# A three-layer kernel whose first stage becomes one written list of single-engine steps, with the retention state summed in PSUM

## The chip, the cores and the metric

One core of a Trainium2 chip runs the kernel. The metric is the device time in microseconds (us) of one execution; a lower number is better. Engine names are those of the profile: PE is TensorE (PEld its weight loads), DVE VectorE, ACT ScalarE, POOL GpSimd, SP SyncE, which here issues almost all DMA transfers. One profiled execution gives the durations, and three unprofiled runs give the times.

## The reference

The input is q, k, v of 4 sequences x 8 heads x 576 positions x 64 dimensions, and the weights of two dense layers.

```python
gamma = 1.0 - 2.0 ** (-5.0 - np.arange(H))            # one decay per head
Dmat = np.where(rel >= 0, gamma ** rel, 0.0)          # rel = position of q - position of k
x = (q @ k.T / sqrt(D) * Dmat) @ v                    # retention; 2304 tokens x 512
h = x @ w_in                                          # 512 -> 1024
solu = h * softmax(h)
ln = (solu - mean) / sqrt(var + 1e-6) * g_ln
x = ln @ w_out                                        # 1024 -> 512
h = x @ w_in2                                         # 512 -> 2048
g = where(h >= 1, h, where(h <= -1, 0, (h + 1)**2 / 4))
out = g @ w_out2                                      # 2048 -> 512
```

The weights arrive as 64-bit floating point words. The chip's engines take them apart as pairs of 32-bit integers ("decoding") and each number is then split into a high and a low part; a product is the sum of three matmuls (low-high, high-low, high-high).

## The kernel before, in words

The 2304 tokens are 18 tiles of 128; a sequence is 4.5 tiles, so tile number modulo 9 is 0 or 4 where a sequence begins, and in tile 4 it begins in the middle.

The kernel has two stages. The **first stage** holds the retention (`ret_scores`, `ret_out`), the first dense layer with its normalisation (`mlp1_hidden`, `mlp1_norm`, `mlp1_transpose`), its output product (`mlp1_out`), and the decoding of all weights: `prep_w_in1` and `prep_w_out1` for the first layer, `prep_w2` for the second layer, whose split weights are stored to DRAM. The **second stage** begins behind the last tile's transposes (`hidden`, `factors`, `project`) and loads these weights again for each block of 512 tokens.

Retention of a tile: PE makes the scores of two heads at a time (L117), DVE multiplies them by a table `in_sb` of decays that is zero above the diagonal (L126), POOL multiplies q by a table (L130) and k by another (L133). PE adds the state of earlier tiles (L145) and the tile's own part (L151) in one PSUM bank `po`, which ACT and DVE split into high and low (L74, L75 by `split`). The next state is the old one times a decay (POOL L182, or ACT L174) plus k times v (PE L172 into a bank `pst`, DVE L185; L179 where a sequence begins). The state lies in SBUF.

First layer of a tile: 12 matmuls of 512 columns for each half of the hidden units (L252), the maximum (DVE L257), exponential (ACT L267), product (DVE L268), squares (ACT L275), the inverse root (POOL L281, L282), scaling (ACT L285), 8 transposes (PE L298), a split, and for each pair of tiles 96 matmuls of 256 columns (L318).

Decoding of one unit of 128 x 512 numbers: ACT scales the high words (L199) and the low words (L200), DVE shifts (L201), POOL adds (L202), DVE merges (L204), ACT and DVE or POOL split. There are 48 such units, of which 16 belong to the first layer.

What sets the order: up to tile 3's hidden half the string `START` gives the order of calls, then a loop over pairs of tiles, with `PACE` as the number of weight units between the calls. Only the queues of SP (in `START`), and of PE and SP (afterwards), keep the written order (`manual_schedule`); on the other engines a planner orders the instructions with its own costs. The 8 PSUM banks are four pairs named `sc`, `o`, `tr`, `h`, each reused in turn.

Of the kernel before, what the change touches and what calls it, by code (L numbers as in the profile page):

```python
# [31 lines left out]
PACE = [[], [0, 0, 0, 0], *[[2, 1, 1, 1]] * 4, *[[2, 2, 1, 1]] * 2, [0, 0, 0, 0]]  # L32

START = """
L0 G0 L1 s0 A0 G1 O0 S1 L2 o1 A1 L3 S2 o2 A2 L4 S3 A3 O3 L5 S4 B0 O4 L6 S5 b1 O5 L7 B2 S6 O6 H0 H1 L8 b3 S7 O7 N0 L9 B4 S8 O8 b5 H2 H3 L10 S9 O9 N1 B6 b7 L11
# [3 lines left out]
def shape_constants():  # L39

    gamma = 1.0 - 2.0 ** (-5.0 - np.arange(H, dtype=np.float64))
    g = gamma.reshape(KD, 2).T
    i = np.arange(P)
    lag = (i[None, :] - i[:, None])[:, None, None, :]
    inside = np.where(lag >= 0, g[None, :, :, None] ** np.maximum(lag, 0), 0.0) / np.sqrt(D)
    before = np.repeat(g[:, :, None] ** (i + 1.0) / np.sqrt(D), D, 0)
    after = gamma[None, :] ** (P - 1.0 - i[:, None])
    across = np.repeat(g ** float(P), D, 0)  # L50
    return [np.ascontiguousarray(x, np.float32) for x in (inside, before, after, across)]
# [3 lines left out]
def net(ctx: ExitStack, tc: tile.TileContext, qk_t, kv, w_in1, w_out1, g_ln, w_in2, w_out2, inside, before, after, across, out):  # L55
# [5 lines left out]
    ps = mlp1.enter_context(tc.tile_pool(name="ps", bufs=2, space=PSUM))  # L61
# [4 lines left out]
    small = ctx.enter_context(tc.tile_pool(name="small", bufs=4, side="right"))  # L66
# [19 lines left out]
    in_sb = at.tile([P, 2, KD, P], F32, name="in_sb", bufs=1)  # L86
    bef_sb = at.tile([P, KD, P], F32, name="bef_sb", bufs=1)
    aft_sb = at.tile([P, H], F32, name="aft_sb", bufs=1)
    acr_sb = at.tile([P, KD], F32, name="acr_sb", bufs=1)
    state = at.tile([P, KD, P], F32, name="state", bufs=1)  # L90
    nc.gpsimd.memset(state, 0.0)
    raws, scaled, x1, probs = {}, {}, {}, {}

    def load_inside(e):
        nc.sync.dma_start(in_sb[:, e], inside[:, e])

    def load_consts(i):
        for x, src in (((aft_sb, after), (bef_sb, before)), ((acr_sb, across), (g_sb, g_ln)))[i]:
            nc.sync.dma_start(x, src)

    def load_qkv(t):
        x = raw.tile([P, 2, KD, P], F32, tag="qk", name="qk")
        y = raw.tile([P, 2, H, D], F32, tag="kv", name="kv")
        nc.sync.dma_start(x, qk_t[t])
        for e in range(2 if t == 0 else 0):
            load_inside(e)
        nc.sync.dma_start(y, kv[t])
        raws[t] = x, y

    def ret_scores(t, alt=False):  # L110
        r = t % RPT
        qk, kv_ = raws[t]
        sc = [ps.tile([P, KD, P], F32, tag="sc", name=f"sc{e}") for e in range(2)]
        for c in range(KD):
            for e in range(2):
                rows = slice(e * D, (e + 1) * D)
                nc.tensor.matmul(sc[e][:, c, :], qk[rows, 1, c, :], qk[rows, 0, c, :], start=True, stop=True)  # L117
        for e in range(2):
            pt = at.tile([P, KD, P], F32, tag=f"p{e}", name=f"p{e}", bufs=1)
            if r == 4:  # L120
                nc.gpsimd.memset(pt[:D, :, D:], 0.0)
                parts = ((slice(0, D), slice(0, D)), (slice(D, P), slice(0, P)))
            else:
                parts = ((slice(0, P), slice(0, P)),)
            for j, i in parts:
                nc.vector.tensor_tensor(out=pt[j, :, i], in0=sc[e][j, :, i], in1=in_sb[j, e, :, i], op=ALU.mult)  # L126
            probs[t, e] = pt
        if r:
            qs = at.tile([P, KD, P], F32, tag="qs", name="qs")
            nc.gpsimd.tensor_tensor(out=qs, in0=qk[:, 0, :, :], in1=bef_sb, op=ALU.mult)  # L130
            scaled[t] = qs
        if r != RPT - 1:
            (nc.vector if alt else nc.gpsimd).tensor_tensor(  # L133
                out=kv_[:, 0, :, :], in0=kv_[:, 0, :, :], in1=aft_sb.unsqueeze(2).to_broadcast([P, H, D]), op=ALU.mult
            )

    def ret_out(t, alt=False):
        r = t % RPT
        _, kv_ = raws.pop(t)
        po = ps.tile([P, KD, P], F32, tag="o", name="po")  # L140
        n_in = 0 if r == 0 else D if r == 4 else P
        if n_in:
            qs = scaled.pop(t)
        for c in range(KD if n_in else 0):
            nc.tensor.matmul(  # L145
                po[:, c, :n_in], state[:, c, :], qs[:, c, :n_in], start=(c == 0), stop=False, skip_group_check=True
            )
        for c in range(KD):
            for e in range(2):
                rows = slice(e * D, (e + 1) * D)  # L150
                nc.tensor.matmul(  # L151
                    po[rows, c, :], kv_[:, 1, 2 * c + e, :], probs[t, e][:, c, :],
                    start=(c == 0 and n_in == 0), stop=(c == KD - 1), skip_group_check=True,
                )
# [7 lines left out]
        xh, xl = x[:, 0], x[:, 1]  # L162
        split(xh, xl, po)
        x1[t] = (xh, xl)
        if r != RPT - 1:
            k0 = D if r == 4 else 0
            pst = ps.tile([P, KD, P], F32, tag="o", name="pst")
            kf = kv_[:, 0, :, :].rearrange("p h d -> p (h d)")
            vf = kv_[:, 1, :, :].rearrange("p h d -> p (h d)")
            for c in range(KD):  # L170
                cols = slice(c * P, (c + 1) * P)
                nc.tensor.matmul(pst[:, c, :], kf[k0:, cols], vf[k0:, cols], start=True, stop=True)  # L172
            for c in range(KD if alt and r not in (0, 4) else 0):
                nc.scalar.activation(state[:, c, :], state[:, c, :], AF.Copy, scale=acr_sb[:, c : c + 1])  # L174
            for e in range(2):
                rows = slice(e * D, (e + 1) * D)
                st = state[rows, :, rows]
                if r in (0, 4):
                    nc.vector.tensor_copy(st, pst[rows, :, rows])  # L179
                    continue  # L180
                if not alt:
                    nc.gpsimd.tensor_tensor(  # L182
                        out=st, in0=st, in1=acr_sb[rows, :].unsqueeze(2).to_broadcast([D, KD, D]), op=ALU.mult
                    )
                nc.vector.tensor_tensor(out=st, in0=pst[rows, :, rows], in1=st, op=ALU.add)  # L185
# [6 lines left out]
    def decode(st, tag=None, sb=False, dst=None):  # L192

        lo, hi = st[:, :, 0], st[:, :, 1]
        y = stage.tile([P, 512], U32, tag="y", name="y", bufs=3)
        w = ps.tile([P, 512], U32, tag=tag, name="w") if tag else y
        nc.scalar.activation(w.bitcast(F32), hi.bitcast(F32), AF.Copy, scale=2.0**-112)  # L199
# [442 lines left out]
```

## Time and profile before

| | us |
|---|---|
| three runs | 722.74, 725.28, 725.74 |
| median of the runs | 725.28 |
| the profiled execution, span from its first to its last instruction | 723.5 |
| a time of its own for the profiled execution, beside its span | not given |
| start of tile 16's transposes, with which the second stage begins | 326.64 |

In windows a line gives each engine's busy time with the count of its instructions, then the granted clock of TensorE as a share of its full speed, the share of the DMA engines' time and the rate. A group of instructions names line, engine, operation and tiles; "x36 | 24.4, 684" is 36 instructions, 24.4 us busy, 684 ns for a mean one; behind the second bar stands the engine's idle time before them and what ended it.

### The profile page before, as it was taken

How to read it: one execution, taken by the hardware profiler on the slowest of the kernel's cores; microseconds unless marked ns; L12 is line 12 of the kernel's file. 1: busy time of each engine (PE TensorE's matmuls, PEld its weight loads, DVE VectorE, ACT ScalarE, POOL GpSimd, SP SyncE). 2: the span in 40 equal slices, each digit the busy share in tenths (PEclk: the TensorE clock that was granted, in tenths of full speed). 3: DMA queues.
4: the chain of work that ended last, by engine and by line, in shares of the span. 5: the costliest groups of instructions: out<-in, count | busy, mean ns of one | idle time of the engine just before them, and what ended most of it. 6: DMA issues, size and time to landing. Idle time of an engine off the chain costs nothing.

```text
span 723.5 us, 12170 instructions
## 1 busy us (share of the span) xinstructions
PE 685.8 (95%) x4744; PEld 617.0 (85%) x4744; DVE 498.1 (69%) x961; ACT 359.9 (50%) x658; POOL 169.0 (23%) x186
## 2 busy tenths in 40 slices
PE   5798878898989999999999999999999999999997
PEld 5687777787878889998889898898989899899996
DVE  3967877678688688755566567655865668575875
ACT  2746784565567578753334343433433343344342
POOL 3895665536545245300000000000000000000000
PEclk9979999899999999999999999999999999999999
DMA  8946536387869499699554513445134511555192
GB/s 309 368 182 231 190 133 195 94 338 270 303 203 345 156 349 411 221 406 403 174 223 167 192 77 146 143 164 219 59 125 182 204 58 66 197 201 194 72 326 111
DMA packets 34825, 152.05 MB, mean 210 GB/s; under 512 B 3792, under 2 KB 11984, under 8 KB 29008
## 3 DMA queue, kind: packets, MB, share of 16 engines
q1 hardware_dynamic: 34624, 151.02, 56.6%
q8 instruction: 37, 0.61, 0.3%
q10 hardware_dynamic: 144, 0.26, 0.1%
q14 instruction: 20, 0.16, 0.1%
HBM read 114.04 MB, written 37.22 MB: 209 GB/s over the span
## 4 chain that ended last, share of the span: by engine, by line
PE 72%; DVE 11%; DMA 7%; ACT 5%; issue 3%; POOL 2%; SPq 1%; DVEq 0%; ACTq 0%; POOLq 0%
PE h L416 27%; PE hp L252 9%; PE px L318 7%; PE pa L464 7%; PE pb L464 7%; PE pc L464 7%; PE pd L464 3%; DMA st<-in_w_in 2%; DMA st<-in_w_out 1%; DVE y L201 1%; POOL y L202 1%; DMA wod<-wo 1%; PE po L151 1%; DVE y L204 1%; PE tp L298 1%
## 5 line engine op out<-in xcount | busy, mean ns | idle before, releaser
L416 PE MATMUL h<-xs,wi 128*128 128x512 f32 (+1 forms) x960 | 214.2, 372 | 0.0
L416 PEld LDWEIGHTS h<-xs,wi 128*128 128x128 f32 x960 | 163.8, 188 | 28.5
L426 DVE SCALAR_TENSOR_TENSOR r<-r 128x512 f32<-128x512 f32 (+1 forms) x80 | 50.8, 635 | 104.0 <-ACT r L424 103.9
L424 ACT ACTIVATE r<-h 128x512 f32<-128x512 f32 (+1 forms) x80 | 44.3, 554 | 154.7 <-PE h L416 154.5
L74 ACT ACTIVATE gh<-gs 128x1024 fp32r<-128x1024 f32 (+1 forms) x80 | 66.9, 874 | 77.1 <-DVE gs L439 72.9
L318 PE MATMUL px<-ln,wo 128*128 128x256 f32 x864 | 101.0, 278 | 0.0
L318 PEld LDWEIGHTS px<-ln,wo 128*128 128x128 f32 x864 | 100.1, 188 | 0.8 <-issue 0.2
L252 PE MATMUL hp<-wi1h,x 128*128 128x512 f32 x288 | 94.9, 412 | 0.0
L75 DVE TENSOR_TENSOR gl<-gs,gh 128x1024 fp32r<-128x1024 f32 (+1 forms) x80 | 77.0, 995 | 13.3 <-ACT gh L74 13.2
L202 POOL TENSOR_TENSOR y<-y,st 128x512 int32<-128x512 int32 x48 | 64.8, 1352 | 65.8 <-ACT st L200 21.7
L464 PE MATMUL pb<-wo,gh 128*128 128x256 f32 x288 | 73.9, 280 | 0.4 <-DVE x L75 0.4
L252 PE MATMUL hp<-wi1l,x 128*128 128x512 f32 x144 | 61.4, 427 | 12.8 <-DVE e L268 10.8
L252 PEld LDWEIGHTS hp<-wi1h,x 128*128 128x128 f32 x288 | 57.4, 199 | 12.8
L439 DVE TENSOR_TENSOR gs<-gs 128x256 f32<-128x256 f32 (+1 forms) x160 | 60.0, 396 | 3.6
L464 PE MATMUL pa<-wo,gh 128*128 128x256 f32 x288 | 62.5, 280 | 0.0
L464 PE MATMUL pc<-wo,gh 128*128 128x256 f32 x288 | 62.0, 280 | 0.0
L431 DVE TENSOR_TENSOR gs<-h,r 128x512 f32<-128x512 f32 (+1 forms) x80 | 51.0, 638 | 7.3 <-DVE r L426 0.5
L464 PEld LDWEIGHTS pb<-wo,gh 128*128 128x128 f32 x288 | 54.3, 188 | 0.6 <-issue 0.6
L464 PEld LDWEIGHTS pa<-wo,gh 128*128 128x128 f32 x288 | 49.2, 188 | 2.7
L464 PEld LDWEIGHTS pc<-wo,gh 128*128 128x128 f32 x288 | 49.1, 188 | 0.0
L252 PEld LDWEIGHTS hp<-wi1l,x 128*128 128x128 f32 x144 | 28.8, 200 | 20.4 <-DVE e L268 11.5
L425 ACT COPY h<-h 128x512 f32<-128x512 f32 (+1 forms) x80 | 43.1, 539 | 0.0
(88 smaller groups left out, 1141.3 us busy)
## 6 DMA issues: line engine op xcount, KB each, us to landing
wo<-wod SPq DMA_DIRECT2D x28, 1792.0 KB, 7.4
wod<-wo SPq DMA_DIRECT2D x8, 1792.0 KB, 9.3
st<-in_w_out SPq DMA_DIRECT2D x24, 512.0 KB, 5.7
qk<-in_qk_t SPq DMA_DIRECT2D x18, 512.0 KB, 6.6
kv<-in_kv SPq DMA_DIRECT2D x18, 512.0 KB, 4.4
xsd<-x SPq DMA_DIRECT2D x36, 256.0 KB, 6.5
st<-in_w_in SPq DMA_DIRECT2D x16, 512.0 KB, 6.0
wid<-wi SPq DMA_DIRECT2D x16, 512.0 KB, 7.4
```

Source lines behind the costliest of these rows:

```text
L74: nc.scalar.activation(hi, src, AF.Copy)
L75: eng.tensor_tensor(out=lo, in0=src, in1=hi.bitcast(F32), op=ALU.subtract)
L202: nc.gpsimd.tensor_tensor(out=y.bitcast(I32), in0=y.bitcast(I32), in1=lo.bitcast(I32), op=ALU.add)
L252: nc.tensor.matmul(hp, a[:, kk, :], w[:, fs], start=(n == 0), stop=(n == 3 * KD - 1))
L318: nc.tensor.matmul(px[:, mm, :], w[:, ms], a[:, f, :], start=(n == 0), stop=(n == 3 * C1 - 1))
L416: nc.tensor.matmul(hp[:, :n], wi[c][:, w, kk], xs[b][:, a, kk], start=(k == 0), stop=(k == 3 * KD - 1))
L424: nc.scalar.activation(r[:, :n], hp[:, :n], AF.Relu, bias=0.5, scale=0.5)
L425: nc.scalar.copy(h[:, :n], hp[:, :n])
L426: nc.vector.scalar_tensor_tensor(out=r[:, :n], in0=r[:, :n], scalar=1.0, in1=r[:, :n], op0=ALU.min, op1=ALU.mult)
L431: nc.vector.tensor_tensor(out=g, in0=h_, in1=r_, op=ALU.max)
L439: nc.vector.tensor_tensor(out=g[:, o], in0=g[:, x], in1=g[:, y], op=op)
L464: nc.tensor.matmul(po[key][:, half], a[:, x, t], wo[p][0][:, w, y], start=(begin and j == 0), stop=(last and j == 2), skip_group_check=True,)
```

## The change

Three things change together; the second stage's functions are the same.

First, the first stage becomes steps of a single engine each, called from one written list `ORDER` of 1130 words, such as `H.8.0.1` (hidden product of tile 8, half 0, into bank 1). All engines and SP keep the order of this list. The planner, `START` and `PACE` are gone from this stage. The words for one weight unit are l (load), a, b, c, d, e (decoding), f, g (split), h (differences), s (store); for one tile q, k (loads), V, S, P, I, O, U, W, D, X, Y (retention) and H, R, m, E, M, z, Q, x, w, r, N, T, K, L (layer); J, G, B, t make the output product and store it; C, i, Z load constants and second-stage data.

Second, v is multiplied by the decay of its position to a negative power (V), the products of k and v are summed in PSUM bank 7 over the tiles of a sequence (U) and copied to SBUF for the next tile (W), and the sum of state and own part is multiplied by the decay of its own position at the end (D). The score mask holds only 0 and 1.

Third, the PSUM banks are named one by one in the list: 0 to 6, bank 7 being the sum. `small` has 3 buffers instead of 4, the loads of the first layer's weights come as halves.

```diff
-PACE = [[], [0, 0, 0, 0], *[[2, 1, 1, 1]] * 4, *[[2, 2, 1, 1]] * 2, [0, 0, 0, 0]]
-START = """
-L0 G0 L1 s0 A0 G1 O0 S1 L2 o1 A1 L3 S2 o2 A2 L4 S3 A3 O3 L5 S4 B0 O4 L6 S5 b1 O5 L7 B2 S6 O6 H0 H1 ...
+ORDER = """
+C.6 l.6 q.0 k.0 q.1 l.2 l.5 l.0 l.3 k.1 a.6.0 l.11 C.1 b.6 c.6 l.4 S.0.1.2 l.14 d.6 l.8 C.5 C.0 V.0 e.6 C.3 q.2
+P.0 f.6 l.7 U.0 C.2 C.4 g.6 S.1.3.4 b.2 W.0 a.2.5 I.1.6 a.5.1 c.2 O.0.2 q.3 b.5 c.5 d.2 a.0.0 P.1 k.2 b.0 d.5
...
+e.23 l.31 T.5.1.5 K.4.0 d.29 l.30 T.4.1.0 G.1.1 L.4.0 I.12.4 K.5.1 B.1.1 h.23.0 K.4.1 H.8.0.1 L.5.1 t.1.1 h.23.1
...
+H.16.1.1 K.14.0 r.15 s.40 G.6.1 L.14.0 N.15.0 B.6.1 N.15.1 t.6.1 K.14.1 T.15.0.0 R.16.1 T.15.1.3 K.15.0 L.14.1
+H.17.1.6 K.15.1 L.15.0 Z.2 L.15.1 m.16 E.16.0 J.7.1.4 R.17.1 E.16.1 m.17 M.16.0 E.17.0 M.16.1 E.17.1 M.17.0
+M.17.1 z.17 x.17 Q.17.0 z.16 x.16 Q.17.1 J.7.0.0 G.7.1 w.17 Q.16.0 r.17 B.7.1 Q.16.1 t.7.1 N.17.1 w.16 r.16
+N.17.0 N.16.0 G.7.0 N.16.1 B.7.0 t.7.0
+"""
-    ps = mlp1.enter_context(tc.tile_pool(name="ps", bufs=2, space=PSUM))
+    ps = mlp1.enter_context(tc.tile_pool(name="ps", bufs=1, space=PSUM))
+    def bank(b, shape, dtype=F32):
+        return ps.tile(shape, dtype, tag=f"b{b}", name="bank")
+    total = bank(7, [P, KD, D])
+    @step
+    def C(i):
+        if i <= MID:
+            nc.sync.dma_start(dec_sb[i], decay[i])
+        elif i == MID + 1:
+            nc.sync.dma_start(g_sb, g_ln)
+        else:
+            nc.scalar.dma_start(mask_sb, masks)
+    @step
+    def V(t, alt=False):
+        v = kvs[t][:, 1]
+        row = MID + 1 if r == 4 else MID if r == 8 else r % MID
+        (nc.vector if alt else nc.gpsimd).tensor_tensor(
+            out=v, in0=v, in1=grow_sb[:, row].unsqueeze(2).to_broadcast([P, H, D]), op=ALU.mult)
+    @step
+    def P_(t):
+        m = mask_sb[:, P : 2 * P] if t % RPT == 4 else mask_sb[:, :P]
+        for e, sc in enumerate(scs.pop(t)):
+            probs[t, e] = at.tile([P, KD, P], F32, tag=f"p{e}", name=f"p{e}", bufs=1)
+            nc.vector.tensor_tensor(out=probs[t, e], in0=sc, in1=m.unsqueeze(1).to_broadcast([P, KD, P]), op=ALU.mult)
+    @step
+    def I(t, b):
+        n = D if t % RPT == 4 else P
+        pos[t] = bank(b, [P, KD, P])
+        for c in range(KD):
+            for e in range(2):
+                rows = slice(e * D, (e + 1) * D)
+                nc.tensor.matmul(
+                    pos[t][rows, c, :n], states[t - 1][rows, c, :], qks[t][rows, 0, c, :n],
+                    start=(c == 0), stop=False, skip_group_check=True)
+    @step
+    def U(t):
+        k0 = D if t % RPT == 4 else 0
+        for c in range(KD):
+            for e in range(2):
+                kf, vf = (kvs[t][k0:, i, 2 * c + e, :] for i in range(2))
+                nc.tensor.matmul(
+                    total[e * D : (e + 1) * D, c, :], kf, vf,
+                    start=(c == 0 and t % RPT in (0, 4)), stop=(c == KD - 1), skip_group_check=True)
+    @step
+    def W(t):
+        states[t] = at.tile([P, KD, D], F32, tag="state", name="state", bufs=2)
+        nc.scalar.copy(states[t], total)
+    @step
+    def D_(t):
+        r = t % RPT
+        xf[t] = at.tile([P, KD, P], F32, tag="xf", name="xf", bufs=1)
+        po = pos.pop(t)
+        for cols, i in ((slice(0, D), MID), (slice(D, P), 0)) if r == 4 else ((slice(0, P), MID if r == 8 else r % MID),):
+            nc.vector.tensor_tensor(out=xf[t][:, :, cols], in0=po[:, :, cols], in1=dec_sb[i][:, :, cols], op=ALU.mult)
+    @step
+    def X(t):
...
+        x1[t] = x[:, 0], x[:, 1]
+        nc.scalar.activation(x[:, 0], xf[t], AF.Copy)
+    @step
+    def Y(t, alt=False):
+        xh, xl = x1[t]
+        (nc.vector if alt else nc.gpsimd).tensor_tensor(out=xl, in0=xf.pop(t), in1=xh.bitcast(F32), op=ALU.subtract)
...
+    with tc.manual_schedule():
+        for word in ORDER.split():
+            name, *args = re.split("[.]", word.rstrip("+"))
+            f = steps[name] if name in steps else steps[name + "_"]
+            f(*map(int, args), *[True] * word.endswith("+"))
...
+    transposes(NT - 2, 4)
+    hidden(0, 0, ps, "b0")
+    hidden(0, 1, ps, "b1")
+    transposes(NT - 1, 6)
```

The steps that are not shown hold the same instructions as the functions they come from: a to g those of `decode` and `split`; H, R, m, E, M, z, Q, x, w, r, N, T, K, L those of the layer's functions; J, G, B, t those of `mlp1_out` and `store_x2`.

## Rows read from the trace of the kernel before

**Rows 1.** The page: busy time, share of the span and instructions of each engine.
```profile
PE 685.8 (95%) x4744; PEld 617.0 (85%) x4744; DVE 498.1 (69%) x961; ACT 359.9 (50%) x658; POOL 169.0 (23%) x186
```
**Rows 2.** Windows: first stage whole, its parts, one stretch, the second stage.
```profile
0.00:326.64 326.64, 294.64 (x2160) 260.47 (x2161) 239.26 (x491) 207.05 (x402) 168.96 (x186) 0.96 0.71 262
0.00:245.00 245.00, 213.00 (x1590) 185.35 (x1591) 182.54 (x362) 148.16 (x284) 141.61 (x152) 0.94 0.65 233
245.00:326.64 81.64, 81.64 (x573) 75.12 (x572) 56.72 (x129) 58.88 (x119) 27.34 (x34) 1.00 0.90 346
200.00:240.00 40.00, 37.73 (x271) 33.41 (x272) 33.98 (x70) 27.76 (x54) 20.11 (x21) 0.96 0.66 239
353.10:723.50 370.40, 364.69 (x2414) 332.62 (x2412) 243.18 (x445) 141.41 (x237) 0.00 (x0) 1.00 0.43 159
```
**Rows 3.** The chain that ended last, in order of time: start, us, what.
```profile
279.29 0.87 PE tp L298 x8
280.16 5.61 PE hp L252 x24
...
292.24 10.89 PE px L318 x96
```
**Rows 4.** Timeline of PE: start, us, engine, line, operation, count.
```profile
138.47 1.16 PE L172 MATMUL pst<-kv 128*128 128x128 f32 x8
139.38 11.16 PE L318 MATMUL px<-ln,wo 128*128 128x256 f32 x96
...
230.91 1.06 PE L145 MATMUL po<-qs,state 128*128 128x128 f32 x8
231.90 1.09 PE L151 MATMUL po<-p,kv 128*64 128x128 f32 x16
232.92 1.16 PE L172 MATMUL pst<-kv 128*128 128x128 f32 x8
234.01 1.16 PE L117 MATMUL sc<-qk 64*128 64x128 f32 x16
```
**Rows 5.** Waits: who waited for whom, us in total, times, longest.
```profile
PE hp L252 <- DVE e L268: 10.8, 4, 4.9
PE sc L117 <- DMA qk<-in_qk_t: 4.5, 1, 4.5
ACT y L199 <- DMA st<-in_w_in: 16.4, 7, 4.9
```
**Rows 6.** Groups of instructions of the first stage, by line and shape.
```profile
L126 DVE TENSOR_TENSOR p<-sc,in_sb 128x512 f32<-128x512 f32 x32 | 20.6, 681 | 0.0
L75 DVE TENSOR_TENSOR x<-po,x 128x512 fp32r<-128x512 f32 x18 | 12.3, 686 | 1.9 <-ACT x L74 1.6
L185 DVE TENSOR_TENSOR state<-pst,state 64x256 f32<-64x256 f32 x24 | 10.0, 417 | 0.7 <-ACT state L174 0.3
L179 DVE COPY state<-pst 64x256 f32<-64x256 f32 x8 | 3.3, 419 | 2.3 <-POOL kv L133 2.3
L130 POOL TENSOR_TENSOR qs<-qk,bef_sb 128x512 f32<-128x512 f32 x16 | 20.9, 1308 | 15.6 <-DMA qk<-in_qk_t 15.2
L182 POOL TENSOR_TENSOR state<-state,acr_sb 64x256 f32<-64x256 f32 x20 | 13.9, 696 | 4.2 <-PE po L145 3.5
L200 ACT ACTIVATE st<-st 128x512 int32<-128x512 uint32 x48 | 32.3, 673 | 3.4 <-DMA st<-in_w_out 2.1 <-DMA st<-in_w_in 1.3
L285 ACT ACTIVATE e<-e,sm 128x512 f32<-128x512 f32 x36 | 27.3, 809 | 7.2 <-POOL sm L282 7.2
L275 ACT ACTIVATE junk<-e,sm 128x512 bf16<-128x512 f32 x36 | 25.9, 719 | 14.9 <-DVE sm L271 14.5
L267 ACT ACTIVATE e<-hp,sm 128x512 f32<-128x512 f32 x36 | 24.4, 684 | 16.3 <-DVE sm L263 16.3
L267 ACT ACTIVATION_READ_ACCUMULATOR e<-hp,sm 128x1 f32 x36 | 7.2, 199 | 0.0
L74 ACT ACTIVATE x<-po 128x512 fp32r<-128x512 f32 x18 | 10.6, 589 | 12.6 <-PE po L151 12.5
```

More of the change, by code (lines that the diff above doesn't have):

```diff
@@ L97, in load_consts @@
[L97 to L110, printed above, removed]
-        r = t % RPT
[L112 to L147, printed above, removed]
+    steps = {}
+    def step(f):
+        steps[f.__name__] = f
@@ L148, in ret_out, with S @@
+    @step
+    def S(t, a, b):
+        scs[t] = sc = [bank(x, [P, KD, P]) for x in (a, b)]
         for c in range(KD):
@@ L161, in ret_out @@
             x = w2a.tile([P, 2, KD, P], F32R, tag=f"w{slot - 2}", name="x1")
[L162 to L185, printed above, removed]
@@ new lines, in net, with l @@
+    wod = [dram.tile([P, 2, 7, 2 * P], F32, name=f"wod{p}") for p in range(C2 // 2)]
+    units = [(0, i) for i in range(2 * KD)] + [(1, f) for f in range(C1)]
+    units += [(2 + w, i) for p in range(C2 // 2) for w in (0, 1) for i in (2 * p, 2 * p + 1)]
+    raw_w, wd, yd, rd, w_in1_sb, wo1, ws, w2x = {}, {}, {}, {}, [None] * KD, [None] * (C1 // 2), {}, {}
+    @step
+    def l(u):
+        kind, i = units[u]
+        if kind == 0:
+            raw_w[u] = boot.tile([P, 512, 2], U32, tag="st", name="st", bufs=6)
+            src = words(w_in1[i // 2 * P : (i // 2 + 1) * P, :], F1)[:, i % 2 * 512 : (i % 2 + 1) * 512]
+        else:
+            raw_w[u] = stage.tile([P, DM, 2], U32, tag="st", name="st")
+            src = words(w_in2[i] if kind == 2 else (w_out1, None, w_out2)[kind - 1][i * P : (i + 1) * P, :], DM)
+        nc.sync.dma_start(raw_w[u], src)
@@ new lines, in a, with b, c @@
+    @step
+    def a(u, b=None):
+        yd[u] = stage.tile([P, 512], U32, tag="y", name="y", bufs=3)
+        wd[u] = yd[u] if b is None else bank(b, [P, 512], U32)
+        nc.scalar.activation(wd[u].bitcast(F32), raw_w[u][:, :, 1].bitcast(F32), AF.Copy, scale=2.0**-112)
+    @step
+    def b(u):
+        lo = raw_w[u][:, :, 0]
+        nc.scalar.activation(lo.bitcast(I32), lo, AF.Copy, scale=2.0**-29)
+    @step
+    def c(u):
+        nc.vector.tensor_scalar(yd[u], wd[u], 3, None, op0=ALU.logical_shift_left)
@@ new lines, in d, with e @@
+    @step
+    def d(u):
+        nc.gpsimd.tensor_tensor(
+            out=yd[u].bitcast(I32), in0=yd[u].bitcast(I32), in1=raw_w[u][:, :, 0].bitcast(I32), op=ALU.add
+        )
+    @step
+    def e(u):
+        kind, i = units[u]
+        w, y, st = wd.pop(u), yd.pop(u), raw_w.pop(u)
+        r = y
+        if kind < 2 and u % 2 == 0:
+            r = w
+        elif kind == 3:
+            if i % 2 == 0:
+                ws[i // 2] = prep.tile([P, 7, 2 * P], F32, tag="ws", name="ws")
+            r = ws[i // 2][:, i % 2 * 2 : i % 2 * 2 + 2].rearrange("p i f -> p (i f)").bitcast(U32)
@@ new lines, in f @@
+    @step
+    def f(u, part=0):
+        kind, i = units[u]
+        if kind == 0 and w_in1_sb[i // 2] is None:
+            w_in1_sb[i // 2] = [w1i.tile([P, F1], F32R, tag=f"w{w}{i // 2}", name=f"wi1{w}") for w in "hl"]
+        if kind == 1 and wo1[i // 2] is None:
+            wo1[i // 2] = w1o.tile([P, 2, 2, DM], F32R, tag=f"w{i // 2}", name="wo1")
+        if kind == 2:
+            w2x[u] = prep.tile([P, 2, DM], F32R, tag="wi", name="wi", bufs=2)
+        if kind == 3 and part == 0:
+            w2x[u] = prep.tile([P, 2, 7, 2 * P], F32R, tag="wo", name="wo")
+        hi, _, r = parts_of(u, part)
+        gain = g_sb[:, i : i + 1] if kind == 1 else 1.0
+        if kind == 1 and u % 2:
+            nc.scalar.activation(r, r, AF.Copy, scale=gain)
+            gain = 1.0
+        nc.scalar.activation(hi, r, AF.Copy, scale=gain)
@@ new lines, in g, with h @@
+    @step
+    def g(u, part=0):
+        kind, i = units[u]
+        hi, lo, r = parts_of(u, part)
+        if kind == 1 and u % 2 == 0:
+            nc.vector.scalar_tensor_tensor(
+                out=lo, in0=r, scalar=g_sb[:, i : i + 1], in1=hi.bitcast(F32), op0=ALU.mult, op1=ALU.subtract
+            )
+        else:
+            (nc.gpsimd if kind < 2 and u % 2 else nc.vector).tensor_tensor(
+                out=lo, in0=r, in1=hi.bitcast(F32), op=ALU.subtract
+            )
+    @step
+    def h(u, n):
+        y = ws[units[u][1] // 2]
+        o, x, z = ((4, 1, 0), (1, 3, 1), (5, 3, 4), (6, 2, 5))[n]
+        nc.gpsimd.tensor_tensor(out=y[:, o], in0=y[:, x], in1=y[:, z], op=ALU.subtract)
@@ L245, in mlp1_hidden, with s, H_ @@
+    @step
+    def s(u):
+        kind, i = units[u]
+        x = w2x.pop(u).bitcast(F32)
+        if kind == 2:
+            nc.sync.dma_start(wid[i], x.rearrange("p w (c f) -> p w c f", c=KD))
+        else:
+            nc.sync.dma_start(wod[i // 2], x)
+    lnT, hps, es, tps, pxs, x2s = {}, {}, {}, {}, {}, {}
+    @step
+    def H_(t, f, b):
         xh, xl = x1[t]
-        hp = ps.tile([P, 512], F32, tag="o" if t == 2 or t >= 13 and t % 2 else "h", name="hp")
+        hps[t, f] = hp = bank(b, [P, 512])
@@ new lines, in N, with T_, columns @@
+    @step
+    def N(t, f):
+        rs, nb = sm(t, 10, 11)
+        nc.scalar.activation(half_of(t, f), half_of(t, f), AF.Identity, bias=nb, scale=rs)
+    @step
+    def T_(t, f4, b):
+        e = es[t][1]
+        tps[t, f4] = bank(b, [P, 4, P])
+        for j in range(4):
+            i = 4 * f4 + j
+            nc.tensor.transpose(tps[t, f4][:, j, :], e[:, i * P : (i + 1) * P], ident)
+    def columns(t, f4):
+        cols = slice((t % 2) * P, (t % 2 + 1) * P)
+        return [x[:, 4 * f4 : 4 * f4 + 4, cols] for x in lnT[t // 2]]
@@ L499, in net @@
     gs = {}
-    start = {
-        "L": load_qkv, "G": load_consts, "S": ret_scores, "O": ret_out, "A": prep_w_in1, "B": prep_w_out1,
-        "H": lambda i: mlp1_hidden(i // 2, i % 2), "N": mlp1_norm, "Y": mlp1_transpose,
-    }
-    order = ExitStack()
-    with tc.manual_schedule(engines={nc.sync.engine}):
-        for step in START.split():
-            start[step[0].upper()](int(step[1:]), *[True] * step[0].islower())
-    order.enter_context(tc.manual_schedule(engines={nc.tensor.engine, nc.sync.engine}))
@@ new lines, in i, with Z @@
+    @step
+    def i(c):
+        load_wi(c, w2a, f"w{c}")
+    @step
+    def Z(n):
+        nonlocal prep, xsa, gsp, wos
+        if n == 1:
+            attn.close()
+            xsa, gsp = (
+                ctx.enter_context(tc.tile_pool(name=x, bufs=1, side="left", reuse_waits="tile")) for x in ("xsa", "gsp")
+            )
+            load_xs(0, xsa)
+            return
+        pre.close()
+        if n == 0:
+            prep = pre.enter_context(tc.tile_pool(name="prep", bufs=1, side="right", reuse_waits="tile"))
+        else:
@@ L564, in net @@
+    order = ExitStack()
+    order.enter_context(tc.manual_schedule(engines={nc.tensor.engine, nc.sync.engine}))
     for c in range(4, 12):
```

410 lines of the change are left out of this document (196 added, 214 removed).

## Prediction

> **What bounds the kernel now.** First the page's engine sums [rows 1]: PE is busy for 95% of the span, DVE for 69%, ACT for 50%, POOL for 23%. That is an average over two stages, so the windows come next [rows 2]. In the second stage, from 353.10 us on, PE works 364.69 of 370.40 us at full clock; this code isn't touched, and its span is taken over as it is. In the first stage the reader is to see two halves. From 245.00 to 326.64 us PE is busy without a gap at clock 1.00. Up to 245.00 us it is busy for 213.00 us, so it idles for 32.0, and the granted clock is only 0.94. No other engine is full there either: over the whole first stage DVE is busy for 239.26 of 326.64 us (73%), ACT for 207.05 (63%), POOL for 168.96 (52%). Nobody is the bound; the engines wait for each other. The waits [rows 5] show it: PE waits 4 times, 10.8 us in all, for DVE's product on a hidden bank, and 4.5 us at the start for the first q and k.
>
> What PE needs if it never waits follows from the dense part. The chain of waits shows 24 hidden matmuls in 5.61 us, 96 of the output product in 10.89 and 8 transposes in 0.87 [rows 3]; so H costs 2.80 us, J 5.45, T 0.435. The timeline, from start to start, gives 0.99 us for L145 (230.91 to 231.90), 1.02 for L151 and 1.09 for L172 before scores, 0.91 before `px`; the scores are about 1.1 [rows 4]. Up to 326.64 us PE has 36 H (100.8), 16 J (87.2), 32 T (13.9), 18 scores (19.8), 18 own parts (18.4), 16 L172 (16.0 at 1.0) and 16 L145 (15.8): 271.9 us of work. The stage loses 54.7 us, of which 32.0 are idle and the rest are work under a lowered clock or thinly issued. A new order can win from these 54.7 us and from nothing else.
>
> **The retention, part by part.** DVE loses the 18 subtractions on `x` (12.3 us), the state's additions (10.0) and copies (3.3) [rows 6]. It gains 18 D of a PSUM and an SBUF operand of 128x512, as L126 at 0.681: 12.3. That is 13 us less, 239 to 226. POOL loses the products on q (20.9) and on the state (13.9) and gains 18 Y; the nearest row is L130's 1.308 us, so 23.5: 11 us less, of which some extra V take back three or four. ACT gains 16 W, a PSUM copy of 128x256: below the 0.589 us of the 128x512 copy `x<-po` and above half of it, 0.29; I take 0.45, so 7 us more. X stays a copy of 128x512.
>
> On PE, I takes L145's place with 16 small matmuls instead of 8 large ones. It can't be dearer than the 1.1 us of the scores, which are also 16 with 64 rows, and half of that (0.55) is the lower end; I take 1.0, since each pair of heads still streams 128 columns. U takes L172's place with 16 matmuls like L151's but of 64 columns: between 0.51 and 1.02, taken as 0.75. PE's sum falls to 100.8 + 87.2 + 13.9 + 19.8 + 18.4 + 16.0 + 12.0 = 268.1 us. The ends of both make this 257 to 274. So the retention by itself moves PE's work by only -4 us; its chain from state to state gets shorter (one ACT copy instead of a POOL product and a DVE addition), while the chain from own part to hidden product gets one step longer (D, X, Y instead of two). Before the dense part the old chain costs PE a few waits at most; I book nothing for either. The 0/1 mask changes no shape and costs nothing.
>
> One rule speaks against the finer retention. PE's L172 takes 1.09 us where scores of 64 rows follow and 0.91 where `px` of full shape follows [rows 4]: 0.18 us at a change of shape. The new list has 90 changes of shape among its 152 PE steps, the old order at most four for each tile, 72. The Trainium skill, TensorEngine Tiling (Array Packing), Tiling Modes, says that changing the mode drains the engine. By that the sum below is 18 x 0.18 = 3 us higher. I leave these 3 us out, because I and U are already taken near their middle or upper ends.
>
> **The list.** I cut it at `H.8.0.1`, about where the words for decoding thin out. Before it stand, on PE, 12 H, 4 J, 11 T, 12 S, 11 O, 12 I and 12 U: 105.6 us. On ACT stand 26 a and 26 b at 0.673 (35.0), 53 copies of f (27, four words have two), K, G and X at 0.589 (31.2), 12 exponentials, squares and scalings at 0.684, 0.719 and 0.809, the first two with an accumulator read of 0.199 (31.3), and 12 W (5.4): 102.9 us. DVE has 187 instructions there, at the stage's mean of 239.26/491 = 0.487 us 91 us, and POOL 75 at 168.96/186 = 0.908, 68 us. Four engines have similar loads and depend on each other, in a fixed order on each. Behind the cut PE has 162.5 us of work, ACT and DVE less.
>
> How full can an engine be that waits for others? The fullest stretch of the old stage is 200 to 240 us: DVE 33.98 of 40 (85%) and PE 37.73 (94%) [rows 2]. I give ACT DVE's 85% up to the cut: 102.9/0.85 = 121.1 us. ACT itself never shows more than 58.88/81.64 = 72% in these rows, but there PE was the bound; at 72% it would be 142.9 us. I give PE its 94.3% behind the cut: 162.5/0.943 = 172.3 us (162.5 where it never waits, as in 245 to 326). The start stays at 4.5 us, as SP still sends one weight unit and then q and k.
>
> At the end, `N.16.1` stands on ACT behind `G.7.0`, which waits for PE's last J. So the second transpose of tile 16 waits for 0.59 + 0.81 us, less the first one's 0.44: 1.0 us new. The hidden product into bank 0 waits for G and B (0.59 + 0.69), which is over by then.
>
> Sum: 4.5 + 121.1 + 172.3 + 1.0 = 298.9 us instead of 326.64: 27.7 us won. The span goes from 723.5 to 695.8. The median of the three runs, 725.28, lies 1.8 above the span; so I predict **698 us**.
>
> What covers what: SP issues the loads in list order. The first hidden product (`H.1.0.1`) needs ten transfers of 512 KB and one of 256 KB before it, 5.5 MB, 16 us at the 346 GB/s of the last window; ACT needs longer to decode them, so this is hidden. From `J.5.1.6` on SP moves 5 loads, 7 stores (three of 1792 KB), 6 t, 3 i, and the second stage's first data, about 22.5 MB, beside 61 us of PE work: 65 us at 346 GB/s, with the DMA engines already 90% busy there. Most of it is needed later, so I book 0, and 4 us as the upper end. The third buffer count of `small` costs nothing while N of a tile comes before the third next R.
>
> **Rivals.**
> 1. The list keeps PE fed and PE's work is the bound: 4.5 + 105.6 + 162.5 + 1.0 = 273.6, 53 us won, 672 us at best. For it: all sums but PE's are below that. Against it: no window of the old stage has two engines over 90%. Half-way between this and the forecast is 685; I call the case 672 to 686.
> 2. ACT stays at 72% up to the cut: 22 us of the gain go, 720 us. For it: E, Q and N wait for DVE and POOL in every tile. Six more bank waits of 2.7 us (10.8/4) would give 714 in the same way, since seven named banks serve everything.
> 3. No change: the time won early returns as waits of T for N later; 725 us.
> 4. Slower: ACT's fixed order makes late weight words block it. Step a waits for its load, and K, E, N and G queued behind it wait as well, then PE. In the old order ACT waits 7 times for `st<-in_w_in`, 16.4 us, 2.3 each [rows 5], and the planner put other work ahead. With 32 units of the second layer to decode, it turns slower from 27.7/2.3 = 12 waits on the path; 18 of them give 698 + 41 = 739 us.
>
> **Numbers.** Forecast 0.58 (own range 687 to 712), rival 1 0.15, rival 2 0.10, rival 3 0.06, rival 4 0.11. About 0.5%, 3.6 us, is what a measurement can tell from no change. Rivals 1 and 2 and the forecast are faster: 0.83; same 0.06; slower 0.11. From 680 to 722 some 0.07 are left out below and 0.13 above.
>
> **What would show it.** In the new profile the first transposes of tile 16 start near 299 us, and `H.8.0.1` near 126; PE's idle time falls from 32 to about 15 us, most of it ahead of `H.8.0.1`, and the granted clock before 245 us rises. DVE's busy sum falls by some 13 us. I and U cost 1.0 and 0.75 us for each tile. The second stage keeps its 370 us from the first projection on. The prediction is wrong if ACT shows more than 20 us of waits for loads, if `H.8.0.1` starts after 145 us, or if PE idles behind it for over 20 us.

## The result and the profile after

The changed kernel takes 703.39 us (median of 4 runs, 702.32 to 704.70), the kernel before beside it 724.01: ratio 0.9707, 95% interval 0.9670 to 0.9743. Forecast were 698 us and a range of 680 to 722. The profiled execution's span fell from 723.5 to 702.9 us. The page's engine sums, which answer to [rows 1]:

```profile
PE 673.8 (96%) x5000; PEld 603.4 (86%) x5000; DVE 483.6 (69%) x926; ACT 364.6 (52%) x666; POOL 161.8 (23%) x166
```

No engine's share says where 20.6 us went. The windows after, which answer to [rows 2], do (columns as there):

```profile
12.00:30.00 18.00, 8.41 (x97) 7.29 (x91) 13.85 (x24) 14.04 (x25) 15.80 (x13) 0.68 1.03 394
0.00:48.00 48.00, 31.86 (x350) 26.85 (x351) 32.19 (x53) 30.06 (x53) 34.77 (x34) 0.86 0.88 327
48.00:126.00 78.00, 75.36 (x735) 64.53 (x734) 59.15 (x133) 60.42 (x122) 43.30 (x45) 1.00 0.70 246
0.00:245.00 245.00, 226.22 (x2083) 196.15 (x2084) 187.93 (x368) 172.03 (x331) 144.17 (x145) 0.97 0.79 281
0.00:130.87 130.87, 112.09 (x1132) 95.91 (x1132) 95.70 (x188) 92.26 (x178) 82.50 (x83) 0.95 0.77 276
130.87:295.77 164.90, 164.90 (x1287) 146.09 (x1286) 128.63 (x269) 118.56 (x232) 79.34 (x84) 1.00 0.84 302
329.05:702.90 373.85, 368.41 (x2413) 336.28 (x2411) 242.25 (x443) 141.52 (x237) 0.00 (x0) 1.00 0.42 154
```

PE's idle time up to 245 us fell from 32.0 us to 18.8 (the fourth line), and 16.1 us of it lie in the first 48 us (the second line). The granted clock up to 245 us rose from 0.94 to 0.97. From 12 to 30 us the DMA engines are full, POOL is busy for 88% and PE for 47% at clock 0.68. From 48 us on PE is nearly full at clock 1.00. All waits of PE in this execution (in each line: us in total, times, longest):

```profile
PE bank L195 <- DMA qk<-in_qk_t: 12.5, 4, 6.1
PE bank L225 <- POOL kv L185: 4.5, 1, 4.5
PE h L565 <- issue: 3.9, 1, 3.9
PE bank L236 <- POOL kv L185: 1.7, 3, 0.6
PE bank L472 <- ACT e L464: 1.0, 1, 1.0
PE pa L613 <- DVE gl L136: 0.2, 1, 0.2
```

The wait for DVE's product on a hidden bank (10.8 us in [rows 5]) is gone. The third line is new and lies behind the first stage. PE's timeline shows its place; where [rows 2] has the border at 326.64 us, it is now at 295.77:

```profile
295.77 0.60 PE L472 MATMUL bank<-ident,e 128*128 128x128 f32 x4
297.32 0.66 PE L472 MATMUL bank<-ident,e 128*128 128x128 f32 x4 [0.95 <-ACT e L464]
297.73 5.70 PE L565 MATMUL h<-xs,wi 128*128 128x512 f32 x24
...
312.37 2.95 PE L565 MATMUL h<-xs,wi 128*128 128x512 f32 x12
315.15 5.63 PE L502 MATMUL bank<-ln,wo 128*128 128x256 f32 x48
324.69 4.57 PE L565 MATMUL h<-xs,wi 128*128 128x512 f32 x12 [3.90 <-issue]
329.05 0.34 PE L613 MATMUL pa<-wo,gh 128*128 128x256 f32 x1
```

The reader is to see 3.90 us of nothing, and twelve matmuls that take 4.57 us instead of 2.95: after the 3.90 us without work the granted clock is 0.63 on average from 324.69 to 329.26, a mean between its two levels (1.2 GHz is 0.50, 2.4 GHz 1.00). DVE's timeline shows what was late:

```profile
319.88 4.10 DVE L136 TENSOR_TENSOR gl<-gs,gh 128x1024 fp32r<-128x1024 f32 x4 [0.70 <-ACT gh L135]
323.90 0.69 DVE L519 TENSOR_TENSOR x<-bank,x 128x512 fp32r<-128x512 f32 x1
```

L519 is step B of `output(1, 5)`: the last read of bank 5, over at 324.59. It stands on DVE behind the four splits of the second stage's factors. PE starts 0.10 us later. That this bank is the one into which the second stage's pool puts its hidden tile `h2` is the first theory below.

In the kernel before PE goes over the border without a gap, and its first projection matmul starts at 353.19:

```profile
350.39 2.96 PE L416 MATMUL h<-xs,wi 128*128 128x512 f32 x12
353.19 0.28 PE L464 MATMUL pa<-wo,gh 128*128 128x256 f32 x1
```

The account by stretches, forecast and measured:

| stretch | before | forecast | after |
|---|---|---|---|
| start to `H.8.0.1` | – | 125.6 | 130.87 |
| `H.8.0.1` to tile 16's transposes | – | 172.3 | 164.90 |
| the two together | 326.64 | 297.9 | 295.77 |
| from there to the first projection | 26.55 | 27.55 | 33.28 |
| first projection to the end | 370.31 | 370.31 | 373.85 |
| outside the span | 1.8 | 1.8 | 1.8 |

The profiled execution is one of the four and took 704.70 us, 1.8 more than its span; the median lies 1.3 us lower. So 30.9 us were won in the first stage, and 6.7 + 3.5 given back in the second, whose code is the same.

### The profile page after: what moved, and what is told of

It is laid out like the page before. It is cut to its first block, busy times and chain, and to the rows that moved or that the text cites. A ratio compares the mean times of both kernels' runs of the same rounds, so it can differ in the third digit from the quotient of the medians.

```text
span 702.9 us, 12647 instructions
## 1 busy us (share of the span) xinstructions
PE 673.8 (96%) x5000; PEld 603.4 (86%) x5000; DVE 483.6 (69%) x926; ACT 364.6 (52%) x666; POOL 161.8 (23%) x166
## 4 chain that ended last, share of the span: by engine, by line
PE 90%; DMA 7%; issue 1%; DVE 1%; ACT 0%; POOL 0%; SPq 0%; DVEq 0%; POOLq 0%; ACTq 0%
PE h L565 29%; PE bank L400 14%; PE bank L502 13%; PE pa L613 7%; PE pb L613 7%; PE pc L613 7%; PE pd L613 4%; DMA qk<-in_qk_t 4%; PE bank L195 2%; PE bank L225 2%; PE bank L472 2%; PE bank L213 2%; DMA kv<-in_kv 2%; DMA st<-in_w_out 2%; PE bank L236 1%
## 5 line engine op out<-in xcount | busy, mean ns | idle before, releaser
L502 PE MATMUL bank<-ln,wo 128*128 128x256 f32 x864 | 102.1, 278 | 0.0
L502 PEld LDWEIGHTS bank<-ln,wo 128*128 128x128 f32 x864 | 100.4, 188 | 1.2
L400 PE MATMUL bank<-wi1h,x 128*128 128x512 f32 x288 | 90.6, 396 | 0.0
L310 POOL TENSOR_TENSOR y<-y,st 128x512 int32<-128x512 int32 x48 | 66.6, 1390 | 53.9 <-DVE y L306 27.6
L400 PEld LDWEIGHTS bank<-wi1h,x 128*128 128x128 f32 x288 | 54.7, 190 | 11.6
L613 PE MATMUL pc<-wo,gh 128*128 128x256 f32 x288 | 63.5, 283 | 0.0
L400 PE MATMUL bank<-wi1l,x 128*128 128x512 f32 x144 | 59.7, 415 | 0.0
L613 PE MATMUL pa<-wo,gl 128*128 128x256 f32 x144 | 40.7, 283 | 0.2 <-DVE gl L136 0.2
```

Source lines behind the costliest of these rows:

```text
L310: nc.gpsimd.tensor_tensor(out=yd[u].bitcast(I32), in0=yd[u].bitcast(I32), in1=raw_w[u][:, :, 0].bitcast(I32), op=ALU.add)
L400: nc.tensor.matmul(hp, a[:, kk, :], w[:, fs], start=(n == 0), stop=(n == 3 * KD - 1))
L502: nc.tensor.matmul(px[:, mm, :], w[:, ms], a[:, f, :], start=(n == 0), stop=(n == 3 * C1 - 1))
L613: nc.tensor.matmul(po[key][:, half], a[:, x, t], wo[p][0][:, w, y], start=(begin and j == 0), stop=(last and j == 2), skip_group_check=True,)
```

## The experiments

Ratios are to the kernel before, with 95% intervals.

**The same kernel again**, for its spread.

> The changed kernel once more, unchanged. Its second stage, from the first projection matmul to the end of the span, took 373.9 us in the first trace of it, against 370.3 us in the kernel before, though nothing of that stage was edited. If that difference belongs to the chip or the execution, this trace shows anything from 370 to 374 us; if it belongs to the kernel, 373.5 to 374.3 us again. Time 703 us, ratio to before 0.971.

702.68 us (0.9709, 0.9670 to 0.9748). The same gap (3.90 us) and a second stage of 373.8 us. `H.8.0.1` starts at 128.58, 2.3 us earlier than in the execution above, and from there to tile 16 it takes 164.89. So the start varies by some 2 us between executions and the rest of the first stage doesn't.

**Another bank for the last output.**

```diff
-    output(1, 5)
+    output(1, 6)
```

> Only the last output product is put into bank 6 instead of bank 5. Theory A (the bank): the 3.9 us for which PE idles at the border of the stages, and the 1.8 us that the next 12 hidden matmuls lose to a lowered clock, come from the second stage's bank for hidden products lying where the last output product lies, which waits for ACT and DVE behind the first factors. Then the gap and the slow matmuls go and the time is 5 to 6 us lower than that of the changed kernel, 697.5 us. Rival B (a load): PE waits for block 0's tokens or weights; then the gap stays at 3.9 us and the time at 703 us.

698.0 us (0.9639, 0.9599 to 0.9678). PE's timeline at the border:

```profile
294.66 0.60 PE L472 MATMUL bank<-ident,e 128*128 128x128 f32 x4
...
319.55 2.96 PE L565 MATMUL h<-xs,wi 128*128 128x512 f32 x12
322.36 0.28 PE L613 MATMUL pa<-wo,gh 128*128 128x256 f32 x1
```

Gap and slow matmuls are gone; from the transposes to the first projection it takes 27.70 us instead of 33.28. Theory A is right; by the address lists of the built programs, `h2` lies in the bank that the list calls 5. The second stage still takes 373.8 us: that loss is another thing.

**`small` with 4 buffers in the changed kernel, with 3 in the kernel before.** All that remains of the change in the second stage is where its tiles lie.

```diff
-    small = ctx.enter_context(tc.tile_pool(name="small", bufs=3, side="right"))
+    small = ctx.enter_context(tc.tile_pool(name="small", bufs=4, side="right"))
```

> The changed kernel with 4 buffers of small instead of 3, as before the change; that moves all later tiles of that side by 48 bytes in each partition. Theory P (place): the second stage's additional 3.5 us come from where its weight tiles lie; then it takes 370.3 us again and the time is 3.5 us lower, 699.5 us. Rival: it is the chip or the execution, or something else in the kernel; then nothing moves beyond 1 us.

> The kernel before with 3 buffers of small instead of 4, and nothing else. Theory P (place): its second stage gets the additional 3.5 us, from 370.3 to 373.8 us, and the time goes to 728 us, ratio 1.005. Rival: nothing moves beyond 1 us, ratio 1.000.

The first gives 700.04 us (0.9668, 0.9629 to 0.9707), its second stage takes 369.8 us instead of 373.8, the gap stays (3.89). The second, the opposite edit in the kernel before, gives 728.3 us (1.0051, 1.0027 to 1.0075), its second stage takes 374.0 instead of 370.3. The projection's group carries the mark: in the changed kernel, and below it in the kernel before with 3 buffers, 283 ns for a mean matmul; then 280 ns in the changed kernel with 4 buffers and, last, in the kernel before.

```profile
L613 PE MATMUL pb<-wo,gh 128*128 128x256 f32 x288 | 75.2, 283 | 0.0
```

```profile
L464 PE MATMUL pb<-wo,gh 128*128 128x256 f32 x288 | 75.2, 283 | 0.4 <-DVE x L75 0.4
```

```profile
L613 PE MATMUL pb<-wo,gh 128*128 128x256 f32 x288 | 73.8, 280 | 0.0
```

```profile
L464 PE MATMUL pb<-wo,gh 128*128 128x256 f32 x288 | 73.9, 280 | 0.4 <-DVE x L75 0.4
```

Theory P holds on both sides: one buffer of 48 bytes fewer, in which no instruction of the second stage takes part, costs 3.7 to 4.0 us there. From the start of one projection matmul to the next the traces show 119.4 ns on average with 3 buffers and 116.7 with 4, in both kernels. 1512 such matmuls at 2.7 ns more are 4.1 us.

**The place itself.** By the address lists of the built programs, the first of the three `wo2` tiles that these matmuls stream begins at byte 86176 of a partition in the fast kernels and at 86240 in the slow ones: 32 and 96 past a multiple of 128, as do the other two. Three kernels move them, all with the last output in bank 6. The first widens the tile in `small` (its pool gave 64 bytes to each buffer before already, so nothing moved); the others put an unused tile behind the pool.

```diff
-            es[t] = (small.tile([P, 12], F32, tag="sm", name="sm"), ...
+            es[t] = (small.tile([P, 16], F32, tag="sm", name="sm"), ...
```

```diff
+    small.tile([P, 16], F32, tag="pad", name="pad", bufs=1)
```

```diff
+    small.tile([P, 24], F32, tag="pad", name="pad", bufs=1)
```

> The last output product in bank 6, and small with 3 buffers of 64 bytes instead of 3 of 48, which puts all later tiles of that side where 4 buffers of 48 put them. Theory P (place): the 256-column matmuls of the projection take 280 ns instead of 283, the second stage loses 3.5 us, and with the 5 us of bank 6 the time is 694 to 695 us. Rival (the number of buffers of small, not the place): 283 ns stay, and the time is that of bank 6 alone, 698 us.

> The last output product in bank 6, small with its 3 buffers of 48 bytes, and 64 unused bytes in each partition behind them. The pool gives each 48-byte buffer 64 bytes, so the try with 64-byte buffers had moved nothing; here the second stage's weight tiles start 64 bytes lower, at 32 bytes past a multiple of 128 instead of 96. Theory P (place): projection matmuls of 280 ns instead of 283, time 3.5 us under bank 6 alone, 694 to 695 us. Rival (the number of buffers of small): 283 ns and 697 to 698 us.

> As the kernel with 64 unused bytes, but with 96: the weight tiles start at a multiple of 128 bytes. If only the distance to a multiple of 128 counts, and zero is the best of them, projection matmuls of 280 ns or less and 694 us or less; if 32 bytes past a multiple is a special place, 283 ns and 698 us.

| kernel | `wo2` at, modulo 128 | mean `pb` matmul | second stage | time | ratio |
|---|---|---|---|---|---|
| wider tile | 86240, 96 | 283 ns | 373.8 | 696.98 | 0.9625 (0.9599 to 0.9652) |
| pad of 64 bytes | 86176, 32 | 280 ns | 370.1 | 694.05 | 0.9581 (0.9548 to 0.9614) |
| pad of 96 bytes | 86144, 0 | 280 ns | 371.1 | 694.86 | 0.9594 (0.9564 to 0.9624) |

The first edit failed to test anything, and says once more that a kernel whose tiles stay keeps its 283 ns. The pads show that the place of the tiles decides. By the address lists the other tiles that move with the pads belong to the first stage alone. The place at 0 is not better than at 32: from start to start 117.6 ns, against 116.8. The pad of 64 bytes beats both kernels; its group reads

```profile
L614 PE MATMUL pb<-wo,gh 128*128 128x256 f32 x288 | 73.9, 280 | 0.0
```

**The order written for PE and SP alone**, the planner for the other engines, as it was before behind `START`.

```diff
-    with tc.manual_schedule():
+    with tc.manual_schedule(engines={nc.tensor.engine, nc.sync.engine}):
```

> The changed kernel, but in the first stage only PE and SP keep the written list's order; ACT, DVE and POOL are ordered by the planner again. Theory L (the list on all engines makes the gain): the planner's order of the other engines brings waits back, tile 16's transposes start 10 to 25 us later than at 295.6 us, and the time is 713 to 728 us. Rival R (the order of PE and SP and the lighter retention make it): tile 16's transposes stay within 4 us of 295.6 us and the time within 700 to 707 us.

741.5 us (1.0232, 1.0200 to 1.0264): slower than before. Windows, the start of the second stage, and two of PE's waits of the first 330 us:

```profile
0.00:48.00 48.00, 29.88 (x314) 25.09 (x314) 30.02 (x48) 29.73 (x52) 33.44 (x33) 0.93 0.85 316
48.00:126.00 78.00, 67.65 (x599) 56.53 (x600) 57.12 (x116) 47.15 (x96) 40.85 (x38) 0.93 0.53 180
126.00:245.00 119.00, 110.60 (x939) 95.55 (x936) 83.36 (x162) 75.39 (x147) 58.06 (x58) 0.99 0.74 259
```

```profile
334.77 5.74 PE L565 MATMUL h<-xs,wi 128*128 128x512 f32 x24 [0.54 <-DVE x L519]
```

```profile
PE bank L472 <- ACT e L464: 5.8, 3, 3.6
PE bank L225 <- POOL wi1l L369: 3.6, 1, 3.6
```

PE's idle time is back, spread over the stage at many small waits for ACT, DVE and POOL; the second stage's first hidden product starts at 334.77 instead of 297.73. With this list on PE, the fixed order on ACT, DVE and POOL is worth 38 us. Theory L is right in direction, and the loss was larger than it said.

**The list with the old retention.** The steps V, I, U, W, D, X, Y do again what the old functions did (q, k and state scaled, score table, the split straight from PSUM). Three kernels differ in when the old tables are loaded: at their words in the list; the table for q at the start on ACT's queue; all three large ones there.

```diff
+            nc.gpsimd.tensor_tensor(out=scaled[t], in0=qks[t][:, 0], in1=bef_sb, op=ALU.mult)
...
-        nc.scalar.copy(states[t], total)
...
+        nc.gpsimd.tensor_tensor(
+            out=states[t], in0=states[t - 1], in1=acr_sb.unsqueeze(2).to_broadcast([P, KD, D]), op=ALU.mult
+        )
+        nc.vector.tensor_tensor(out=states[t], in0=total, in1=states[t], op=ALU.add)
```

> The written list with the old decays: decay table on the scores, q and k scaled on POOL, the state in SBUF scaled by POOL and added by DVE, the split on ACT and DVE straight from PSUM at the place of D. PE's matmul shapes stay those of the changed kernel; the list was not made for these steps. Theory L: the list keeps most of the gain; DVE gets 13 us and POOL 8 to 11 us more, most of it hidden behind PE after 48 us, tile 16's transposes start 0 to 8 us later than at 295.6 us, time 703 to 711 us. Rival R (the sum in PSUM makes the gain): the chain from state to state is back, tile 16's transposes start 15 to 30 us later, time 717 to 732 us.

> The written list with the old decays again. In the first try the table for q was loaded behind six weight units, and PE waited 13.4 us for tile 1's scaled q; here ACT's queue loads this table at the start. If that wait was the whole loss (theory L, the list makes the gain), the time falls by 12 to 18 us, to 711 to 716 us, and what is left above 703 us is what the old decays cost on DVE and POOL in the first 60 us. Rival R (the sum in PSUM makes the gain by itself): other waits for the state take its place and the time stays above 721 us.

> The list with the retention steps of before, as in the run with the early table, but now all three tables of the old decay (the score table of 512 KB, the query table of 256 KB, the value table) start at time 0 on ACT's queue. That is 616 KB more in the first microseconds than the mask of 152 KB. Theory L (the list alone makes the gain, and the old retention lost time in the two runs before only because its tables came late): the single 13 us wait for the first state is gone, under 6 us of it remain, tile 16's transposes start at 303 to 308 us, and the time is 711 to 717 us. Rival R (the old chain itself is what delays: the state passes from tile to tile over DVE and POOL, the scaled queries and values over POOL): TensorE still waits over 12 us in its first 60 us for the state, the scaled queries or the scaled keys although all tables have landed, it waits for POOL later too, and the time is at least 721 us.

728.65 us (1.0052, 1.0033 to 1.0070), 728.4 (1.0055, 1.0035 to 1.0075) and 717.76 (0.9911, 0.9876 to 0.9947). The first two say little about the retention: in the first PE waited 13.4 us for the scaled q, whose table came behind the weights; in the second the same wait came from the next late table. PE's longest wait there, and DVE's that made it:

```profile
PE bank L225 <- DVE state L257: 13.0, 1, 13.0
```

```profile
DVE p L215 <- DMA in_sb<-in_inside: 14.7, 2, 10.8
```

With all tables early that wait is gone. PE's longest waits up to 300 us, that for the state, and the border in its timeline:

```profile
PE bank L203 <- DMA qk<-in_qk_t: 11.8, 3, 6.2
PE bank L227 <- POOL qs L162: 7.8, 3, 3.7
PE bank L239 <- DVE y L341: 3.2, 1, 3.2
PE bank L250 <- POOL kv L195: 1.6, 3, 1.1
PE bank L250 <- DVE state L264: 1.0, 1, 1.0
```

```profile
308.23 0.60 PE L488 MATMUL bank<-ident,e 128*128 128x128 f32 x4
```

Tile 16 starts at 308.23: 18.4 us earlier than before, 12.5 later than after. So the list, with its named banks and its half loads, carries some 18 of the 31 us, and the new retention 12 when the list is there (14 by the medians, 717.76 for 703.39). Both bounds of theory L were missed by a little (717.76 for 717 at most, 308.23 for 308). The wait for the first state is gone, as theory L said, but PE waits 7.8 us for POOL's scaled q. Rival R's state chain is 1.0 us of PE's waits. The truth lies between the theories, nearer to L. The list was written for the new steps; what a list made for the old ones would give wasn't tried, and the larger tables at the start may have a part in the 12 us. Nor were the named banks or the half loads tried by themselves.

**Loads in another order at the start**: q of tile 2 and one decay table before two weight units, the other tables later.

```diff
-... S.0.1.2 l.14 d.6 l.8 C.5 C.0 V.0 e.6 C.3 q.2
-P.0 f.6 l.7 U.0 C.2 C.4 g.6 ...
+... S.0.1.2 q.2 C.0 d.6 l.14 V.0 e.6 l.8
+P.0 f.6 l.7 U.0 C.5 g.6 ... C.2 b.0 d.5 ... C.3 C.4 f.2 ...
```

> Only the order of SP's first transfers: tile 2's q is loaded ahead of two first-layer weight units and four decay tables, and three decay tables come later. In the changed kernel's first 48 us the DMA engines are 88% busy, PE waits 12.5 us for q in all, 5.1 of them for tile 2 at 20.9 us. Theory D (the first 48 us are bound by what is loaded when): tile 2's scores start 4 to 6 us earlier than at 26.0 us, and tile 16's transposes 2 to 5 us earlier, time 698 to 701 us. Rival W (weights' decoding sets the first hidden products): the wait for q goes, PE waits for the same time at the next step, and the time stays at 702 to 704 us.

704.8 us (0.9720, 0.9692 to 0.9748): no gain. PE's waits:

```profile
PE bank L195 <- DMA qk<-in_qk_t: 6.3, 2, 6.0
PE bank L400 <- DVE wi1l L369: 5.7, 1, 5.7
```

6.2 us of waits for q went, and 5.7 for the first weights took their place. Tile 2's scores start at 20.96 us instead of 26.01, as theory D said, but the first hidden product starts at 29.73 instead of 29.92: rival W is right. Whether the loads (the DMA engines are full from 12 to 30 us here too) or the decoding behind them set that start isn't separated by these runs.

## Why the prediction was right, and where it wasn't

**The side and the cause were right.** The list fills PE: from `H.8.0.1` to tile 16 it never idles. It takes the fixed order on all engines for that, as the run with the planner shows. Rivals 3 and 4 are out: ACT's waits for loads of weights in the first 300 us are 12.9 us in 13 small pieces,

```profile
ACT st L302 <- DMA st<-in_w_in: 4.2, 5, 1.2
ACT st L302 <- DMA st<-in_w_out: 4.1, 4, 1.6
ACT bank L297 <- DMA st<-in_w_in: 4.0, 3, 2.3
ACT y L297 <- DMA st<-in_w_in: 0.6, 1, 0.6
```

so the 20 us that would have refuted the forecast weren't reached.

**Behind the cut** I gave PE 94.3% and it has no idle time: 164.9 us, where the sum of work was 162.5. The term was 7.4 us too high: PE's work is the bound there, as rival 1 had it for the whole stage. What I left unbooked, the 0.18 us at a change of shape, has by the prices of my sum no more than the 2.4 us between 164.9 and 162.5 to hide in; no run takes it by itself. The rule of the Trainium skill behind it (TensorEngine Tiling (Array Packing), Tiling Modes) is that a change of mode drains the engine.

**Up to the cut** the sum was 5.3 us short (130.87 for 125.6; 128.58 in the second profile), and its working was wrong in both factors. ACT's work there is 92.26 us, not 102.9, and its share 70%, not 85%. Those errors nearly cancel, so that the sum came this close is luck. Rival 2 had the share right (72%), but not the work that it is a share of. ACT doesn't set the pace either: PE waits for it nowhere there. By the prices of my sum, with the measured I and U, PE has 24.5 us of work before `H.0.1.2`, which starts at 46.62 us, and 79.8 between there and the cut: 22.1 us are lost in the first 46.62 and 4.5 in the 84.25 behind. The step that failed is the filling at the start, "ACT needs longer to decode them, so this is hidden". In its place the DMA engines are full from 12 to 30 us, and PE waits for q and k twice before 46.62 us, 11.2 us in all (12.5 with two later waits), of which I had booked 4.5. For 5.0 us more it waits for POOL's product on v (V), a step of the new retention that stands in the list behind decoding on POOL; I had booked nothing on PE for it. The remaining 6 us of the 22.1 are not idle time: PE's work takes longer there than at my prices, at a granted clock of 0.68 from 12 to 30 us.

**The retention's prices** were close. The groups after, which answer to [rows 6]:

```profile
L213 PE MATMUL bank<-qk,state 64*64 64x128 f32 x224 | 16.2, 286 | 0.1
L236 PE MATMUL bank<-kv 128*64 128x64 f32 x224 | 10.3, 240 | 1.7 <-POOL kv L185 1.7
L252 DVE TENSOR_TENSOR xf<-bank,dec_sb 128x512 f32<-128x512 f32 x16 | 10.9, 683 | 0.9 <-POOL x L269 0.5 <-PE bank L225 0.4
L269 POOL TENSOR_TENSOR x<-xf,x 128x512 fp32r<-128x512 f32 x18 | 23.4, 1297 | 14.1 <-ACT x L264 14.1
L244 ACT COPY state<-bank 128x256 f32<-128x256 f32 x16 | 5.9, 369 | 7.3 <-PE bank L236 6.3 <-PE bank L213 1.0
```

D 0.683 us (0.681 forecast), Y 1.297 (1.308), W 0.369 (0.45); from start to start I takes 1.02 us (129.85 to 130.87 us; 1.0) and U 0.51 to 0.69, most often 0.62 (0.75), behind the first two. DVE's sum fell by 14.5 us (13). What failed is "I book nothing for either": the old retention costs about 12 us more than the new one once the list leaves PE little slack, as the run with all tables early shows. PE's waits there put this on POOL's scaled q (7.8 us) more than on the chain from state to state (1.0), and how much of the rest is slower work isn't shown. The forecast met the sum without it, which is luck too.

**The border.** The 1.0 us for tile 16's second transpose came as 0.95. What failed is the sentence beside it. I checked that bank 0 was free and didn't ask where the next stage's PSUM pool lies: 5.7 us (33.28 for 27.55). And "its span is taken over as it is", said of the second stage, failed by 3.5 us for a reason that no row of before shows. These 9.2 us, less the 2.1 us by which the first stage came earlier than forecast, are the 7.1 us between the forecast span of 695.8 and 702.9. The median, 1.3 us below the profiled execution, is 5.4 us above the forecast of 698.

## What to carry to other kernels

Where no engine is full and all wait for each other, price the list at PE's work behind the filling of the pipeline, and price the filling by itself, from its loads and from the steps that stand behind them on each engine. Where two stages have PSUM pools of their own, look up which bank each first tile of the second stage takes over, and which late read, queued behind what, sets it free. When a stage whose code didn't change gets slower evenly, compare the addresses of its tiles too, not only its instructions.

## What the hardware showed that I had not expected

The same fp32 matmul of 256 columns takes 2.6 to 2.7 ns longer from start to start when the tile it streams begins 96 bytes past a multiple of 128 in its partition than at 32 (119.4 ns for 116.7 to 116.8), and 1.8 ns longer than at 0 (117.6). That is 373.8 to 374.0 us of second stage in four kernels with 96 (the changed one, with bank 6, with the wider tile, and the one before with 3 buffers), and 369.8 to 371.1 in the four with 32 or 0 (the one before, the changed one with 4 buffers, and both pads). Why the address matters is open, and only these three offsets were run. And a gap of 3.90 us on PE cost 5.6: the rest is the lowered clock (0.63) of the twelve matmuls behind it, 4.57 us for 2.95. In the kernel with 4 buffers the same twelve took 5.46 us behind a gap of 3.89, so this price varies between executions.
